# Feature-map attention and a feed-forward block on one core: hand-set slots against a list scheduler that orders all work

## The chip, the cores and the metric

The kernel runs on one core of one Trainium2 chip. Its engines run side by side: PE (TensorE, matrix multiplications), DVE (VectorE), ACT (ScalarE), POOL (GpSimd), and SP, which here only issues DMAs. Each executes its own list of instructions strictly in the order of the program and waits on semaphores for the others. The metric is the device time of one execution in microseconds (us), the median of several runs.

## The reference

Inputs are q, k, v of 8 batches, 8 heads, 576 positions, 64 elements, a matrix omega of 128 features, and weights `w_in` (512 x 2048) and `w_out` (2048 x 512), which arrive as float64.

```
phi(x) = exp(h - max(h)) / sqrt(128),  h = x @ omega.T - |x|^2/2      (x: q or k, scaled by 64**-0.25)
kv = phi(k).T @ v        z = sum over positions of phi(k)             (per batch and head)
attn = (phi(q) @ kv) / (phi(q) @ z + 1e-6)
x = attn as (4608 tokens, 512);   out = gelu(x @ w_in) @ w_out
```

A batch is 576 tokens, and its 8 heads fill the 512 columns of x. So no token of a batch can enter the feed-forward part before all heads of that batch are done.

## The kernel before, in words

**Attention** is cut into 32 units: unit k is batch k // 4 and a pair of heads, j = k % 4. Each unit loads q, k and v, projects k and q with omega on PE, subtracts the row maxima and takes exp (DVE, ACT, POOL), forms kv and z (PE), and divides numerator by denominator on DVE (`div`), which writes columns j of x. Units of batches 0 and 1 are *plain*: float32 matmuls. Those of batches 2 to 7 are *split*: each operand is divided into a high and a low part, which gives cheaper matmuls and more work for the other engines. Units share their buffers (`et`, `kvz`, `qh`), mostly single ones.

**Weights** come in 16 pieces of 1 MB through two buffers `raw`. Each is turned from float64 into float32 (ACT L199 and L203, DVE L209 and L210, POOL L215, result `w32`) and its maximum is taken (L226). When all pieces of a matrix are in, its scale follows, and each of its 16 chunks is split into two float16 halves (`wih`, `wil`; `woh`, `wol`; ACT L235, DVE L250).

**Feed-forward** goes by blocks of tokens, `TBS = (384,) * 10 + (128, 384, 256)`, and in each block by 16 chunks c of 128 hidden features. Block 0 needs no split weights: it multiplies float32 x by float32 `w32` (L937, L989). From block 1 on x is split into `xh` and `xl` (ACT L920, DVE L925, scaled by an exponent that needs the whole batch), the first product takes 12 float16 matmuls a chunk (`mm1`, L953), ACT computes gelu and its high half (L966, L967), DVE its low half `gl` (L976), and the second product takes three matmuls for every 128 tokens of a chunk (`mm2`, L995 to L997). Two PSUM buffers `h` hold first products and are free again after `gl`.

**What sets the order.** Every step is entered as an event with a time: `at(t, fn, ...)`. The times are slots of the feed-forward part (`slot`: 6 per chunk of 384 tokens) plus hand-set offsets from the table `X` (an attention unit's steps lie at fixed distances from a *burst*, one for each unit), and 37 single events are moved by `ADJ`. The events are sorted by time, and in that order the instructions are written out; each engine's list follows from it.

Of the kernel before, what the change touches and what calls it, by code (L numbers as in the profile page):

```python
# [21 lines left out]
SUB = 6  # L22
# [19 lines left out]


TBS = (384,) * 10 + (128, 384, 256)


ADJ = {6: 1.3, 24: -0.12, 25: 0.23, 27: -0.86, 44: -1.17, 46: -0.95, 64: 3.26, 65: -0.06, 67: -0.35,
# [7 lines left out]
def favor_attention_ffn(ctx: ExitStack, tc: tile.TileContext, qT, kT, v, omT, w_in, w_out, out):  # L55

# [26 lines left out]
    MID = S // P  # L83

# [16 lines left out]
    wmax = cp.tile([P, 2, NF // 2], F32, name="wmax")  # L101
    vmax = cp.tile([P, B * NJ], F32, name="vmax")
# [19 lines left out]
    def ps_at():  # L122
        return pp.tile([P, 512], F32, tag="at", name="at", bufs=3)

    def ps_h():
        return pp.tile([P, 512], F32, tag="h", name="h", bufs=2)

    def ps_acc():
        return pp.tile([P, 512], F32, tag="acc", name="acc", bufs=3)

    rot = [0]

    def ps_any():
        rot[0] += 1
        return (ps_at, ps_h, ps_acc, ps_at, ps_acc, ps_h, ps_at, ps_acc)[rot[0] % 8]()

    events = []

    def at(t, fn, *a):
        events.append((t + ADJ.get(len(events), 0), len(events), fn, a))  # L140

    class Obj:
        pass

    own = {}

    def has(u, *ks):
        assert all(own[k] is u for k in ks), (u.b, u.j, ks)

    done, steps = set(), {}  # L150

    def step(o, k):

        assert steps.get(o, 0) == k, (o, k)
        steps[o] = k + 1

    def need(*ks):
        assert all(k in done for k in ks), ks


    wi_raw = w_in.bitcast(I32).rearrange("(j p) w -> p j w", p=P)
    wo_raw = w_out.bitcast(I32).rearrange("(c p) w -> p c w", p=P)
    ep, mp, dp, late = [], [], [], []
    lent = set()

    def p2():

        if not late:
            dp.pop()
            stage.close()  # L170
            pool = ctx.enter_context(tc.tile_pool(name="p2", bufs=1, side="right", reuse_waits="tile"))
            vb = pool.tile([P, NV, VW + 1], F16, name="vb")
            nc.vector.memset(vb[:, :, D:D + 1], 1.0)
            nc.vector.memset(vb[D:P, MID, D:D + 1], 0.0)
            nc.vector.memset(vb[0:D, MID + 1, D:D + 1], 0.0)
            late.extend((pool, vb))
        return late[0]

    def w_load(pc):
        pc.raw = dp[0].tile([P, 2 * pc.n], I32, tag="raw", name="raw", bufs=2)  # L180
        for h, src in enumerate(pc.src):
            dst = pc.raw[:, h * pc.n:(h + 1) * pc.n]
            nc.sync.dma_start(dst.rearrange("p (j w) -> p j w", j=NJ) if pc.win else dst, src)
        pr = pc.raw.rearrange("p (n t) -> p n t", t=2)
        pc.lo, pc.hi = pr[:, :, 0], pr[:, :, 1]

    def w_scale(pc):
        step(pc, 0)


        if X['lsp'] >> (pc.win * 8 + pc.i) & 1 and not (pc.i > 3 and not pc.win):
            k = (pc.win, pc.i + 4) if pc.i < 4 else (False, pc.i)
            assert steps.get(('b',) + k) is None
            pc.l, pc.at = w32[:, k[0], 2 * k[1]:2 * k[1] + 2].rearrange("p c w -> p (c w)"), k
            lent.add(k)
        else:
            pc.l, pc.at = pc.lo, None
        hf = pc.hi.bitcast(F32)
        nc.scalar.activation(hf, hf, AF.Copy, scale=2.0 ** -112)  # L199
        if X['wls'] >> pc.i & 1:  # L200
            nc.gpsimd.tensor_scalar(pc.l, pc.lo.bitcast(U32), 2.0 ** -29, 1.0, op0=ALU.mult, op1=ALU.mult)
        else:
            nc.scalar.activation(pc.l, pc.lo.bitcast(U32), AF.Copy, scale=2.0 ** -29)  # L203

    def w_bits(pc):
        step(pc, 1)
        assert (pc.win, pc.i) not in lent
        step(('b', pc.win, pc.i), 0)
        nc.vector.tensor_scalar(pc.b, pc.hi, 3, None, op0=ALU.logical_shift_left)  # L209
        nc.vector.scalar_tensor_tensor(pc.b, pc.hi, -2 ** 31, pc.b, op0=ALU.bitwise_and, op1=ALU.bitwise_or)  # L210

    def w_round(pc):
        step(pc, 2)

        nc.gpsimd.tensor_tensor(pc.b, pc.b, pc.l, op=ALU.add)  # L215
        lent.discard(pc.at)
        done.update(('w32', pc.win, c) for c in pc.c)

    def w_max(pc):
        step(pc, 3)  # L220
        need(*[('w32', pc.win, c) for c in pc.c])
        if X['wmx'] >> pc.i & 1 and not pc.win:

            nc.scalar.activation(wol[:, 2 * pc.i:2 * pc.i + 2].rearrange("p c w -> p (c w)"), pc.w, AF.Abs, accum_out=wmax[:, pc.win, pc.i:pc.i + 1])
        else:
            nc.vector.tensor_reduce(wmax[:, pc.win, pc.i:pc.i + 1], pc.w, axis=AX.X, op=ALU.max, apply_absolute_value=True)  # L226
        done.add(('wmax', pc.win, pc.i))

    def w_high(pc):
        step(pc, 4)  # L230
        need(('wsc', pc.win))
        s = wsc[:, pc.win, 1:2]
        for x, (w, wh, _) in enumerate(pc.parts):
            if (pc.c[x] % 2, True, False, pc.c[x] % 4 > 0)[X['whp']]:
                nc.scalar.activation(wh, w, AF.Copy, scale=s)  # L235
            else:
                nc.gpsimd.tensor_scalar(wh, w, s, 1.0, op0=ALU.mult, op1=ALU.mult)

    def w_low(pc):
        step(pc, 5)  # L240
        s = wsc[:, pc.win, 1:2]
        for x, (w, wh, wl) in enumerate(pc.parts):
            if pc.c[x] % 4 >= 4 - X['wlp' if pc.win else 'wlq']:
                for h in range(4):
                    t = sp.tile([P, P], F32, tag="wt", name="wt", bufs=1)
                    a, d, e = (y[:, h] if pc.win else y[:, h * P:(h + 1) * P] for y in (w, wh, wl))
                    nc.gpsimd.tensor_scalar(t, a, s, 1.0, op0=ALU.mult, op1=ALU.mult)
                    nc.gpsimd.tensor_tensor(e, t, d, op=ALU.subtract)
# [123 lines left out]
    def xs_pieces(b, half):  # L372
        t0 = b * S + half * HS
        t1 = t0 + HS
        for n in range(NBLK):
            a, e = max(t0, T0[n]), min(t1, T0[n + 1])
            if a < e:
                yield n, a - T0[n], e - T0[n], a - t0
# [859 lines left out]
```

## Time and profile before

| | us |
|---|---|
| time, median of 3 runs (1007.23 to 1007.65) | 1007.6 |
| span of the profiled execution, first to last instruction | 1003.8 |
| outside the span | 3.8 |
| PE busy | 977.9 |
| DVE busy | 727.7 |
| ACT busy | 720.9 |
| POOL busy | 331.3 |

The time of the profiled execution is its span and what lies around it; the page gives the span. A matmul's recorded duration overlaps the next one's, because PE works on several at once, so busy PE is not PE at its peak. What a stream of matmuls costs is read from the distance between the starts of two records; a row of the timeline that ends in "x8" merges eight records. A float32 matmul is two records.

### The profile page before, as it was taken

The page shows a single profiled execution, that of the slowest core. Times are in us where ns is not written, and L with a number is a line of the kernel's source. Part 1 is how long each engine was busy: PE and PEld are TensorE (multiplying, and loading weights), DVE is VectorE, ACT ScalarE, POOL GpSimd, SP SyncE. Part 2 cuts the span into 40 slices and gives each one's busy share as a digit, 9 for nine tenths or more (in the row PEclk, how much of TensorE's full clock was granted, in tenths as well). Part 3 has the DMA queues.
Part 4 walks back from the last instruction along what each step waited for, and adds up shares of the span by engine and source line. Part 5 has one row for each costly group of instructions (what it writes and reads, how often), then busy time and mean ns, then how long its engine had stood idle before and what let it go on. Part 6 is the DMA issues. An engine that isn't in the chain of part 4 may idle for free.

```text
span 1003.8 us, 17322 instructions
## 1 busy us (share of the span) xinstructions
PE 977.9 (97%) x5980; PEld 597.4 (60%) x5980; DVE 727.7 (72%) x1800; ACT 720.9 (72%) x1542; POOL 331.3 (33%) x528
## 2 busy tenths in 40 slices
PE   9999999999999999899999999899999999999998
PEld 6655555566656666466566666456655656565576
DVE  5898777977778888887888779777878877431111
ACT  6876668877777877977787877877788886552333
POOL 1334314323353444343444443443454332100000
PEclk9999999999999999999999999999999999999999
DMA  8766312611211231111421222021121010000000
GB/s 245 211 211 195 120 47 61 186 43 30 79 48 48 80 100 48 43 38 48 121 58 48 69 67 72 24 77 48 49 79 43 26 59 2 22 23 1 1 32 22
DMA packets 50647, 70.91 MB, mean 71 GB/s; under 512 B 18560, under 2 KB 27136, under 8 KB 50560
## 3 DMA queue, kind: packets, MB, share of 16 engines
q1 hardware_dynamic: 50560, 69.81, 24.1%
q8 instruction: 47, 0.77, 0.3%
q14 instruction: 40, 0.33, 0.1%
HBM read 60.36 MB, written 9.44 MB: 70 GB/s over the span
## 4 chain that ended last, share of the span: by engine, by line
PE 75%; ACT 11%; DVE 8%; POOL 3%; issue 2%; DMA 1%; SPq 0%; ACTq 0%; POOLq 0%; DVEq 0%
PE h L953 29%; PE acc L995 10%; PE acc L996 10%; PE acc L997 10%; PE at L712 3%; PE at L445 2%; PE at L479 2%; PE at L632 2%; ACT xh L920 1%; POOL w L215 1%; PE h L937 1%; PE at L816 1%; PE acc L989 1%; ACT gh L967 1%; PE at L777 1%
## 5 line engine op out<-in xcount | busy, mean ns | idle before, releaser
L953 PE MATMUL h<-xh,wih 128*128 128x384 f16 (+2 forms) x768 | 238.3, 314 | 4.9 <-DVE gl L976 4.9
L953 PE MATMUL h<-xl,wih 128*128 128x384 f16 (+2 forms) x768 | 238.2, 313 | 0.0
L953 PE MATMUL h<-xh,wil 128*128 128x384 f16 (+2 forms) x768 | 237.9, 313 | 0.0
L438 POOL TENSOR_TENSOR r<-xt,r 64x256 fp32r<-64x256 f32 (+2 forms) x216 | 164.8, 770 | 216.0 <-ACT r L432 209.4
L995 PE MATMUL acc<-woh,gh 128*128 128x512 f16 (+1 forms) x528 | 198.7, 377 | 0.4 <-ACT o L1006 0.4
L996 PE MATMUL acc<-woh,gl 128*128 128x512 f16 (+1 forms) x528 | 198.4, 376 | 0.1
L997 PE MATMUL acc<-wol,gh 128*128 128x512 f16 (+1 forms) x528 | 198.4, 376 | 0.0
L953 PEld LDWEIGHTS <-wih 128*128 128x128 f16 x1536 | 142.9, 98 | 85.6 <-DVE gl L976 3.3
L976 DVE SCALAR_TENSOR_TENSOR gl<-h,bs,gh 128x384 f16<-128x384 f32 (+2 forms) x192 | 110.7, 578 | 112.2 <-ACT gh L967 109.3
L966 ACT ACTIVATE h<-h,bs 128x384 f32<-128x384 f32 (+2 forms) x192 | 100.9, 527 | 95.6 <-PE h L953 94.4
L432 ACT CAST r<-xt 128x256 fp32r<-128x256 f32 (+2 forms) x216 | 84.6, 404 | 43.1 <-PE at L479 23.3
L967 ACT ACTIVATE gh<-h,bs 128x384 f16<-128x384 f32 (+2 forms) x192 | 105.8, 553 | 3.4
L953 PEld LDWEIGHTS <-wil 128*128 128x128 f16 x768 | 75.2, 98 | 47.4 <-issue 4.6
L997 PEld LDWEIGHTS <-gh 128*128 128x128 f16 x544 | 53.2, 98 | 60.3
L995 PEld LDWEIGHTS <-gh 128*128 128x128 f16 x544 | 52.9, 97 | 43.8 <-ACT gh L967 0.2
L996 PEld LDWEIGHTS <-gl 128*128 128x128 f16 x544 | 53.3, 98 | 41.3 <-issue 0.7
L445 PE MATMUL at<-om,r 128*128 128x256 f32 x216 | 60.5, 352 | 1.5 <-DVE et L464 0.8
L479 PE MATMUL at<-r,om 128*128 128x288 f32 x192 | 56.1, 374 | 1.3 <-DVE et L464 0.8
L725 ACT ACTIVATE dt<-at,vsc 64x288 f32<-64x288 f32 x80 | 39.6, 495 | 21.5 <-PE at L712 20.2
L732 DVE STREAM_TRANSPOSE rt<-dt 128x288 f32<-128x288 f32 x64 | 30.4, 475 | 29.0 <-ACT dt L725 25.7
L550 ACT CAST qh<-qt 128x288 fp32r<-128x288 f32 x96 | 40.5, 433 | 13.5 <-DVE qt L543 13.3
L937 PE MATMUL h<-xs,w 128*128 128x384 f32 x128 | 47.7, 499 | 0.8 <-ACT g L960 0.6
(196 smaller groups left out, 1810.4 us busy)
## 6 DMA issues: line engine op xcount, KB each, us to landing
xt<-in_kT SPq DMA_DIRECT2D x56, 288.0 KB, 4.0
xt<-in_qT SPq DMA_DIRECT2D x56, 288.0 KB, 3.9
out_x<-o SPq DMA_DIRECT2D x35, 256.0 KB, 2.0
raw<-in_w_in SPq DMA_DIRECT2D x16, 512.0 KB, 5.0
raw<-in_w_out SPq DMA_DIRECT2D x16, 512.0 KB, 4.5
w<-in_v SPq DMA_DIRECT2D x5, 1280.0 KB, 7.2
vt<-in_v SPq DMA_DIRECT2D x12, 320.0 KB, 4.1
out_x<-o SPq DMA_DIRECT2D x2, 128.0 KB, 1.7
```

The lines of the kernel that those rows point to most:

```text
L432: nc.scalar.copy(u.r[i][:, 0:b - a], xf[:, a:b])
L438: nc.gpsimd.tensor_tensor(r, xf[D:, a:b], r, op=ALU.subtract)
L445: nc.tensor.matmul(u.pp[i][:, t], r[:, t * P:(t + 1) * P], om, start=True, stop=True)
L479: nc.tensor.matmul(ps[:, 0:HS], om[:, i], r, start=(i == 0), stop=(i == 1))
L937: nc.tensor.matmul(hs[0, c][:, 0:TB[0]], wi32[:, c, j], xs[0, j][:, 0:TB[0]], start=(j == 0), stop=(j == NJ - 1))
L953: nc.tensor.matmul(h[:, 0:TB[n]], w, (xh, xh, xl)[k], start=(i == 0), stop=(i == 3 * NJ - 1))
L966: nc.scalar.activation(g, h, AF.Gelu, scale=bsc[n][:, 2:3])
L967: nc.scalar.activation(gh, g, AF.Copy, scale=bsc[n][:, 3:4])
L976: nc.vector.scalar_tensor_tensor(gl, g, bsc[n][:, 3:4], gh, op0=ALU.mult, op1=ALU.subtract)
L995: nc.tensor.matmul(acc, gh[:, s], woh[:, c, c0:c1], start=(c == 0), stop=False)
L996: nc.tensor.matmul(acc, gl[:, s], woh[:, c, c0:c1], start=False, stop=False)
L997: nc.tensor.matmul(acc, gh[:, s], wol[:, c, c0:c1], start=False, stop=(c == NF - 1))
```

## The change

The table of offsets, the moved events and the sorting are gone. Every step is now an operation `op(engine, cost, function, ..., r=, w=, new=)`: it names what it reads and writes and which new buffers it takes. From that the class `Planner` derives dependencies. Each operation gets a due time, going backwards from its successors, from tables `STARTS` (a time for each block) and `UDUE` (one for each half of each unit), and an offset by kind of step (`OFF`). `Planner.run` then keeps a clock for each engine: whenever an engine is free, it takes, of all operations that are ready and whose buffers are free, the one with the earliest due time. The instructions are written out in that order, before the kernel runs, and pinned on each engine with order-only dependencies (`add_manual_dep`).

The blocks are now `(256, 256) + (384,) * 10 + (256,)`: 13 as before, the float32 block 0 with 256 tokens, and blocks 0 and 1 (512 tokens) lie inside batch 0. The x of both is one tile `xa`. Units 1 and 3 of the first batch use second copies of `et`, `kvz` and `qh` (laid over the place where `w_out` will stand, `flat0`), the first four units may take any of the eight PSUM buffers as they are free, and plain units load q and k into alternating halves of `xt`. The weights' pieces are all of `w_in` first, then all of `w_out`; before, they alternated. What is computed stays the same, step by step.

```
-TBS = (384,) * 10 + (128, 384, 256)
+TBS = (256, 256) + (384,) * 10 + (256,)
...
-    def at(t, fn, *a):
-        events.append((t + ADJ.get(len(events), 0), len(events), fn, a))
...
-    for t, _, fn, a in sorted(events, key=lambda e: e[:2]):
...
-        fn(*a)
+        for o in reversed(self.ops):
+            k, n, x, add = o.own or (0, 0, 0.0, 0.0)
+            o.due = 1e9 if k == 0 else UDUE[n] if k == 2 else add if k == 3 else add + STARTS[n] + ...
+            for s in o.succ:
+                o.due = min(o.due, s.due - o.c - (lat.get(o.e, 0) + hop.get(s.e, 0) if s.e != o.e else 0))
...
+                for o in cand[e]:
+                    t = room(o)
+                    if t is None:
+                        continue
+                    if t > now + 1e-9:
+                        later.append(t)
+                        continue
+                    p = (o.due - bonus.get(o.kind, 0.0), o.id)
+                    if best is None or p < best[0]:
+                        best = (p, o)
...
+            u.eb = j % 2 if b == 0 else int(u.mode == 2 and j % 2 == 0 and u.k > X['eb0'])
...
+    xa = cp.tile([P, NJ, TB[0] + TB[1]], F32, name="xa")
+    qh2 = flat0[:, 2 * NT * M:2 * NT * M + R2]
...
+    def put(o):
+        n = len(nc.cur_bb.bb.instructions)
+        o.fn(*o.a)
+        for i in nc.cur_bb.bb.instructions[n:]:
+            if i.engine in last:
+                tc.add_manual_dep(i, last[i.engine], ...)
```

Three places show how the order moves. The first is PE's list at the end of the float32 block, where the first split block begins. Before (`xs` is x, `acc` a second product, `w` the float32 weights, `et` and `r` parts of an attention unit):

```order
L989 MATMUL acc<-w_71,g 128x512
L479 MATMUL at<-r,om 128x288 x2
L937 MATMUL h<-xs_0_272,w_71 128x384
L937 MATMUL h<-xs_1_418,w_71 128x384
L445 MATMUL at<-om,r 128x256
L937 MATMUL h<-xs_2_516,w_71 128x384
L703 MATMUL at<-qh,kvz 64x288 x4
L937 MATMUL h<-xs_3_624,w_71 128x384
L479 MATMUL at<-r,om 128x288 x2
L989 MATMUL acc<-w_71,g 128x512 x3
L479 MATMUL at<-r,om 128x288 x2
L953 LDWEIGHTS wih
L953 MATMUL h<-xh,wih 128x384
```

and now:

```order
L1035 MATMUL acc<-w_71,g 128x512 x5
L554 MATMUL at<-vt_73,et 128x65 x8
L554 MATMUL at<-vt_73,et 128x130
L1009 MATMUL h<-xa,w_71 128x256 x4
L592 MATMUL at<-ident,et 128x128 x4
L523 MATMUL at<-om_66,xt 128x128 x8
L592 MATMUL at<-ident,et 128x128 x4
L1014 LDWEIGHTS wih
L1014 MATMUL h<-xh,wih 128x256
L1014 LDWEIGHTS wil
L1014 MATMUL h<-xh,wil 128x256
```

The float32 matmuls have 256 columns instead of 384, and the first split block, also of 256 columns, starts while plain units of batch 1 (`om,xt`, `ident,et`) are still in work; before, the last plain unit was just ending (`qh,kvz`) and split units had begun (`r,om`).

The second is DVE's list at the last `xl` of the first block that needs batch 1: block 1 before, block 2 now. Before:

```order
L733 RECIPROCAL rc<-rt 128x9
L490 TENSOR_REDUCE mx<-et 128x9
L734 STREAM_TRANSPOSE rt<-rc 128x288
L250 SCALAR_TENSOR_TENSOR wol<-w_71,wsc,woh 128x512
L740 TENSOR_TENSOR xs_3_642<-at,rt 128x192
L740 TENSOR_TENSOR xs_3_1481<-at,rt 128x96
L488 STREAM_TRANSPOSE et<-at 128x288
L250 SCALAR_TENSOR_TENSOR wol<-w_71,wsc,woh 128x512
L925 SCALAR_TENSOR_TENSOR xl<-xs_3_642,bs,xh 128x384
```

and now:

```order
L761 TENSOR_TENSOR et<-at,lo 128x256
L762 TENSOR_REDUCE nm<-et 128x2
L805 TENSOR_TENSOR ql<-qt,qh 128x288
L1030 SCALAR_TENSOR_TENSOR gl<-h,bs,gh 128x256
L799 STREAM_TRANSPOSE qt<-et 128x288
L805 TENSOR_TENSOR ql<-qt,qh 128x288
L579 RECIPROCAL zr<-zr 128x2
L580 TENSOR_REDUCE km<-at 128x2
L1003 SCALAR_TENSOR_TENSOR xl<-xs,bs,xh 128x384
```

Before, 283 DVE instructions stand up to that `xl`, seven splits of `w_out` (`wol`) are still to come after it, and no `gl` has been computed. Now 347 stand there, among them all sixteen `wol`, fifteen `gl` of block 1, eight maxima of v, and the end of a first split unit (`qt`, `ql`).

The third is DVE's list at a later block's start. Before, at block 4:

```order
L976 SCALAR_TENSOR_TENSOR gl<-h,bs,gh 128x384
L925 SCALAR_TENSOR_TENSOR xl<-w_71,bs,xh 128x384
L732 STREAM_TRANSPOSE rt<-dt 128x288
L488 STREAM_TRANSPOSE w_71<-at 128x288
L733 RECIPROCAL rc<-rt 128x9
L490 TENSOR_REDUCE mx<-w_71 128x9
L734 STREAM_TRANSPOSE rt<-rc 128x288
L925 SCALAR_TENSOR_TENSOR xl<-w_71,bs,xh 128x384
L743 TENSOR_TENSOR w_71<-at,rt 64x288 x2
L502 TENSOR_TENSOR mx<-mx,mc 64x36
L976 SCALAR_TENSOR_TENSOR gl<-h,bs,gh 128x384
```

and now, at block 5, the one that needs batch 3 as block 4 did:

```order
L1003 SCALAR_TENSOR_TENSOR xl<-w_71,bs,xh 128x384 x2
L773 STREAM_TRANSPOSE w_71<-at 128x288
L775 TENSOR_REDUCE mx<-w_71 128x9
L761 TENSOR_TENSOR w_71<-at,lo 128x256
L762 TENSOR_REDUCE nm<-w_71 128x2
L834 SCALAR_TENSOR_TENSOR w_71<-et,w_71 128x256 x2
L761 TENSOR_TENSOR w_71<-at,lo 128x128
L762 TENSOR_REDUCE nm<-w_71 128x1
L834 SCALAR_TENSOR_TENSOR w_71<-et,w_71 128x256
L1030 SCALAR_TENSOR_TENSOR gl<-h,bs,gh 128x384
L773 STREAM_TRANSPOSE w_71<-at 128x288
L1030 SCALAR_TENSOR_TENSOR gl<-h,bs,gh 128x384
```

Before, block 4's `xl` stand one by one between the last `gl` of block 3, with division and maxima of attention units between them. Now they come at up to two in a row and are spread over a longer stretch of attention work, with the `gl` in pairs.

More of the change, by code (lines that the diff above doesn't have):

```diff
@@ L157, in need @@
[L157 to L177, printed above, removed]
@@ L219, in w_max @@
[L219 to L237, printed above, removed]
@@ L239, in w_low @@
[L239 to L248, printed above, removed]
-            else:
-                nc.vector.scalar_tensor_tensor(wl, w, s, wh, op0=ALU.mult, op1=ALU.subtract)
-        done.update(('w', pc.win, c) for c in pc.c)
@@ new lines, in favor_attention_ffn @@
+    ANY = ('at', 'acc', 'h')
+    op('SP', 0, load_om, w=['om32'], size=65e3)
+    op('DVE', 0.6, zeros, w=['z', 'ones', 'vt1s', ('w32', 0, NF - 1)])
+    op('PE', 4.8, warm, r=['z', ('w32', 0, NF - 1)], new=[('h', 'warm')], due=(3, 0, 0.0, -50.0))
+    op('POOL', 0.5, identity, w=['ident'])
+    op('DVE', 0.23, scale_om, w=['om32'])
+    op('DVE', 0.5, split_om, r=['om32'], w=['om'])
+    wi_raw = w_in.bitcast(I32).rearrange("(j p) w -> p j w", p=P)
+    wo_raw = w_out.bitcast(I32).rearrange("(c p) w -> p c w", p=P)
@@ new lines, in v_scales, with v_spread, batch_v @@
+    def v_scales(b):
+        t = G['vsc', b]
+        fields(vexp[:, 0, b:b + 1], t[0:32])
+        mul(nc.gpsimd, t[0:32, 1:2], t[0:32, 0:1], EPS * KSC)
+    def v_spread(b):
+        spread(G['vsc', b])
+    def batch_v(b):
+        us = units[b * NJ:(b + 1) * NJ]
+        op('SP', 0, load_vst, b, w=[u.vk for u in us], size=1311e3)
+        for u in us:
+            op('DVE', 0.8, v_max, u, r=[u.vk], w=[('vm', b)])
+        chain(b, 0)
+        op('POOL', 0.8, v_scales, b, r=[('exp', b, 0)], new=[('vsc', ('vsc', b))])
+        op('ACT', 0.3, v_spread, b, w=[('vsc', b)])
@@ L1202, in favor_attention_ffn, with block @@
[L1202 to L1206 removed]
+    mp.append(ctx.enter_context(tc.tile_pool(name="mp", bufs=1, reuse_waits="tile")))
+    def block(n):
+        block_prep(n)
+        for c in range(NF + LAG):
+            if c < NF:
+                ffn_first(n, c)
+            if c >= LAG:
+                ffn_second(n, c - LAG)
@@ new lines, in favor_attention_ffn @@
+    for u in units[:NJ]:
+        unit_plain(u)
+    chain(0, 1)
+    op(None, 0, nothing, deps=[o for u in units[1:NJ:2] for k in (('kvz', u), ('qh', u)) for o in PL.users[k]],
+       w=[('w32', 0, c) for c in range(8)] + [(x, 1, t) for x, n in (('et', NT), ('eq', 4)) for t in range(n)])
+    for i in range(NF // 2):
+        weights_in(1, i)
+    for i in range(NF // 2):
+        weights_in(0, i)
+    op('DVE', 0.2, p2, w=['p2', 'vb'], deps=[o for w in range(2) for i in range(NF // 2) for o in PL.users['raw', w, i]])
@@ new lines, in favor_attention_ffn @@
+    for c in range(NKK, NF):
+        op(None, 0, nothing, w=[('w32', 1, c), ('xw', c)])
+    done_u = NJ
+    for n in range(1, NBLK):
+        b1 = (T0[n + 1] - 1) // S
+        while done_u < (b1 + 1) * NJ:
+            u = units[done_u]
+            if u.j == 0 and not u.kp:
+                batch_v(u.b)
+            (unit_split if u.split else unit_plain)(u)
+            done_u += 1
+            if u.j == NJ - 1:
+                chain(u.b, 1)
+        block(n)
+    lat = dict(PE=0.18, ACT=0.107, DVE=0.07, POOL=0.046)
```

1549 lines of the change are left out of this document (756 added, 793 removed), and 8 rows, old and new, of tables (ADJ, UDUE).

## The prediction

> **What bounds the kernel now.** I read the page first, then the table by stretches of time, the groups of matmuls, the timeline and the waits.
>
> ```profile
> span 1003.8 us, 17322 instructions
> PE 977.9 (97%) x5980; PEld 597.4 (60%) x5980; DVE 727.7 (72%) x1800; ACT 720.9 (72%) x1542; POOL 331.3 (33%) x528
> PE 75%; ACT 11%; DVE 8%; POOL 3%; issue 2%; DMA 1%; SPq 0%; ACTq 0%; POOLq 0%; DVEq 0%
> ```
>
> PE looks full, but the chain that ended last spends a quarter of the span on other things. So PE's queue and PE's waits both count. What a full stream costs is read from starts in the timeline of PE (start, duration, line, out<-in, shape, count), first in the float32 block, then in a 384-token and in a 256-token block:
>
> ```profile
> 141.06 2.74 PE L937 MATMUL h<-xs,w 128*128 128x384 f32 x8
> 143.73 1.19 PE L703 MATMUL at<-qh,kvz 128*64 128x288 f32 x8
> 144.85 2.84 PE L989 MATMUL acc<-w,g 128*128 128x512 f32 x6
> 147.53 1.45 PE L937 MATMUL h<-xs,w 128*128 128x384 f32 x4
> ...
> 900.07 0.33 PE L953 MATMUL h<-xh,wih 128*128 128x384 f16 x1
> 902.02 0.38 PE L995 MATMUL acc<-woh,gh 128*128 128x512 f16 x1
> ...
> 957.81 0.27 PE L953 MATMUL h<-xh,wih 128*128 128x256 f16 x1
> 959.12 0.38 PE L995 MATMUL acc<-woh,gh 128*128 128x512 f16 x1
> 961.07 0.27 PE L953 MATMUL h<-xh,wih 128*128 128x256 f16 x1
> ...
> 1000.37 0.27 PE L997 MATMUL at<-wol,gh 128*128 128x256 f16 x1
> ```
>
> Twelve float16 matmuls of 384 columns take 902.02 - 900.07 = 1.95 us, 0.163 each; twelve of 256 columns 1.31, 0.109 each; nine of 512 columns 1.95, 0.217 each. Float32 records take 2.67 / 8 = 0.334 (384 columns) and 2.68 / 6 = 0.447 (512 columns), changes of kind included. The counts stand in the groups of PE by shape:
>
> ```profile
> L953 PE MATMUL h<-xh,wih 128*128 128x384 f16 x640 | 209.3, 327 | 4.9 <-DVE gl L976 4.9
> L995 PE MATMUL acc<-woh,gh 128*128 128x512 f16 x512 | 194.3, 380 | 0.4 <-ACT o L1006 0.4
> L445 PE MATMUL at<-om,r 128*128 128x256 f32 x216 | 60.5, 352 | 1.5 <-DVE et L464 0.8 <-POOL r L438 0.7
> L479 PE MATMUL at<-r,om 128*128 128x288 f32 x192 | 56.1, 374 | 1.3 <-DVE et L464 0.8 <-POOL r L438 0.5
> L937 PE MATMUL h<-xs,w 128*128 128x384 f32 x128 | 47.7, 499 | 0.8 <-ACT g L960 0.6 <-DVE xs L740 0.2
> L989 PE MATMUL acc<-w,g 128*128 128x512 f32 x96 | 45.7, 598 | 0.0
> ```
>
> Three groups of 640 and three of 512 like the first two rows are 1920 x 0.1625 + 1536 x 0.217 = 645 us; charging every other group in the same way by its closest spacing (the smaller blocks 42, the float32 block 82, attention 171, the warm-up 5) brings the 5980 records to 945. Of the span, 59 us are no stream of matmuls, more than the 26 of visible idle. Charged by stretches, some 31 of the 59 lie before 190 us, 24 between there and 1000, and 3.4 behind the last matmul.
>
> The table by stretches (start:end, length, then busy time and count of PE, PEld, DVE, ACT, POOL, the granted clock, DMA) shows who is short where:
>
> ```profile
> 0.00:25.00 25.00, 22.62 (x186) 17.12 (x187) 13.72 (x38) 16.83 (x47) 4.15 (x8) 1.00 0.85 245
> 25.00:175.00 150.00, 144.41 (x750) 83.97 (x749) 123.99 (x247) 109.48 (x198) 52.08 (x52) 1.00 0.47 142
> 250.00:400.00 150.00, 148.08 (x901) 91.48 (x899) 123.56 (x325) 115.86 (x260) 64.13 (x108) 1.00 0.25 68
> 400.00:550.00 150.00, 145.05 (x882) 87.21 (x880) 124.17 (x321) 121.45 (x267) 62.79 (x106) 1.00 0.22 60
> ```
>
> The granted clock is 1.00. In 25:175 PE executes 750 records, in 250:400 901; DVE is 83% busy in both. At the start no engine is full: the work waits for weights and for one unit at a time. Later it is the blocks' starts:
>
> ```profile
> PE h L953 <- DVE gl L976: 4.9, 6, 1.4
> PE at L632 <- POOL w L609: 3.7, 4, 1.1
> ...
> 406.82 0.92 DVE L743 TENSOR_TENSOR w<-at,rt 64x288 f32<-64x288 f32 x2
> 407.77 0.19 DVE L502 TENSOR_TENSOR mx<-mx,mc 64x36 f32<-64x36 f32 x1
> 407.99 0.62 DVE L976 SCALAR_TENSOR_TENSOR gl<-h,bs,gh 128x384 f16<-128x384 f32 x1
> 408.53 0.61 DVE L925 SCALAR_TENSOR_TENSOR xl<-w,bs,xh 128x384 f16<-128x384 f32 x1
> ...
> 408.67 0.34 PE L953 MATMUL h<-xh,wih 128*128 128x384 f16 x1 [1.15 <-DVE gl L976]
> ```
>
> Block 4's first matmul at 408.67 waits 1.15 us for a `gl` that stands on DVE behind two divisions; the last attention steps of a batch, the new block's `xh` and `xl` and the old one's `gl` all want the same moment.
>
> **The change part by part.** *Fewer float32 tokens.* For 128 tokens the float32 block spends (128 x 0.334 + 96 x 0.447) / 3 = 28.6 us, or 27.5 by the closest spacing. These tokens move into float16: the block of 128 becomes one of 256. That adds half of 192 x 0.109 + 96 x 0.217, 20.9 us. PE gains 6.6 to 7.7; I take **7**. Other matmuls are the same in number, as are table loads of ACT up to two, so nothing else is removed; DVE has 24 small divisions more (more blocks cut through a unit's tokens), with 24 x about 0.2 = 5 us, beside PE.
>
> The Trainium skill ("TensorE: Matmul & The Clock Gate", back-to-back issue gap) gives two figures for 512 columns, 216 ns by a formula and about 131 ns as the sustained spacing of real streams. By 131 the 48 second products of the added tokens would cost 6.3 instead of 10.4, and the gain would be about 11. This trace has 217, so the sum stays with it.
>
> *The start.* Before, the first split block reaches into batch 1 and needs eight units. Now block 1 ends at token 512 and needs batch 0 alone; block 2 is the first that needs eight units. The comparable points are PE's first matmul of block 1 before and of block 2 now:
>
> ```profile
> 171.16 0.34 PE L953 MATMUL h<-xh,wih 128*128 128x384 f16 x1
> ...
> 173.59 0.61 DVE L925 SCALAR_TENSOR_TENSOR xl<-xs,bs,xh 128x384 f16<-128x384 f32 x1
> ```
>
> Up to there PE's list before amounts to 140 us of stream, reached at 171, so 31 short. Now it holds 77 - 55 = 22 less of the float32 block and 41 more of block 1 and further units: 159. On DVE 283 instructions stand up to that last `xl`, with 137 us busy (the two stretches' 13.72 + 123.99) and 37 idle. Now it is 347 instructions; the 64 more are priced by DVE's groups:
>
> ```profile
> L976 DVE SCALAR_TENSOR_TENSOR gl<-h,bs,gh 128x256 f16<-128x256 f32 x16 | 7.8, 484 | 35.6 <-ACT gh L967 35.6
> L250 DVE SCALAR_TENSOR_TENSOR wol<-w,wsc,woh 128x512 f16<-128x512 f32 x16 | 12.2, 781 | 0.4 <-ACT woh L235 0.4
> L851 DVE TENSOR_REDUCE vmax<-w 128x1 f32<-128x640 f32 x20 | 15.5, 798 | 0.0
> ```
>
> Fifteen `gl` 7.3, seven `wol` 5.5, eight maxima 6.4, and about 10 for parts of split units: 29, of which consecutive instructions overlap a tenth: 27. So DVE must be busy for 164 us before that `xl`, against 159 of PE's stream. **DVE now sets the time of block 2's start**, and its idle time decides: at least the 11 us of the first 25, in which data arrive, at most the 37 it has now. PE is then 164 + 11 - 159 = 16 to 42 short there. A second copy of the first units' tiles and free choice of ready work should remove waits behind a blocked instruction. That eight maxima of v, needed only by batches 3 and 4, stand so early shows that the planner found room on DVE there. But dependencies stay, so I keep 12 of the 26 idle us after the first 25 (DVE 92% busy): 164 + 11 + 12 = 187, 28 short, where PE before is 31 short at the same amount of stream. Gain **3** (bounds -11 and +15).
>
> `w_in` now comes wholly ahead of `w_out` in SP's queue. Up to the last piece of `w_out` there are 16.8 MB of weights and about 7 of q, k, v; at the 245 GB/s of the first stretch that is 97 us, at a fifth less 121, and block 1's second products begin after 118 us of stream and 16 or more of shortfall. The order is covered by that; without the cover it would cost some 10 us for a splitting that can't begin before the last piece is in.
>
> *Later blocks.* Of the 24 us I count some 18 at block starts and 6 as the spread loss of changing between float16 and attention matmuls, which stays. Before, new batches are needed at blocks 1, 3, 4, 6, 7, 9, 11; now at 2, 3, 5, 6, 8, 9, 11, so the starts of 4 and 7, where it waits longest, get free, and 5 and 8 take over their need. A due time for each `gl` and `xl` should shorten waits like the one at 408.67; a planner's clock that is off by a few tenths of a us makes new ones. Bounds: all 18 gone, or 10 more (half again as many). I take **10** gained. The tail (last store) is the same.
>
> Sum: 1003.8 - 7 - 3 - 10 = 983.8, and with the 3.8 by which the median stands above the span, **987.6**.
>
> **The rivals.** *(a) DVE becomes the bound.* Before, DVE reaches its place in the list at a steady rate: 83% busy in each stretch up to 550. If that is set by dependencies which a scheduler can't remove, the early 37 idle us remain, block 2 starts 42 short, 11 more than now, and since block 3 needs 12 units at token 896 (before at 1152) DVE stays behind until block 3's `xl`, for some 8 us more; the later starts gain nothing. 1007.6 - 7 + 11 + 8 = 1020 at most, and about 1014 if a third of the 19 is made up. With the 8 it decides from the point at which DVE is idle for over 27 us ahead of block 2's `xl`. For it: DVE's list is front-loaded now. Against it: a ready list leaves an engine idle only if nothing is ready.
>
> *(b) Only the matmuls count*: the new order waits as often as the old one. 1007.6 - 7 = 1001.
>
> *(c) The scheduler works nearly perfectly*: 16 short at block 2 instead of 31 and 18 gone later, 1007.6 - 7 - 15 - 18 = 968.
>
> *(d) The order isn't executed as planned* (the pinned lists wait at places where the planner's clock is wrong by much): no change within 2 us, with losses that eat the 7.
>
> **How the numbers follow.** Forecast 0.55, its own range 976 to 998; (a) 0.14, (b) 0.15, (c) 0.13, (d) 0.03. The range of 8 in 10 leaves out the slower half of (a) and the faster half of (c): 968 to 1010. A measurement of this kernel tells about 0.2% (2 us) from no change: faster 0.83 (forecast, b, c), the same 0.04, slower 0.13.
>
> **What would show it.** The PE groups should have 64 float32 matmuls (128 records) of 256 columns at about 0.22 between starts, and 64 records fewer of 512 (right for the 7). The first 384-column float16 matmul should start near 187; near 175 speaks for (c), near 200 for (a), with DVE about 92% busy between 25 and 175 in the forecast and 83% in (a). Later, the waits of L953's successor on `gl` should fall from 4.9 to under 3, and a stretch such as 400:550 should hold fewer than 3 us of PE idle instead of 5. The forecast is wrong if PE's idle in the middle rises, or if PE's stream up to block 2 isn't behind DVE but behind ACT or the DMAs of `w_out`.

## The result

The change takes 1009.6 us (median of 20 runs, 1007.7 to 1013.2) against 1007.1 for the kernel before (20 runs, 1004.9 to 1011.2): a ratio of 1.0033, 95% interval 1.0020 to 1.0046. It is 0.3% slower, where 987.6 us and a gain of 2% were forecast. The profiled execution spans 1006.9 us, before 1003.8.

The page of the change, the lines that answer to those of before (span, busy time by engine, the granted clock, which is the share of its full speed that PE's clock was allowed, in tenths for 40 slices, and the chain of waits by engine):

```profile
span 1006.9 us, 17394 instructions
PE 973.8 (97%) x5996; PEld 606.1 (60%) x5996; DVE 777.6 (77%) x1824; ACT 724.7 (72%) x1538; POOL 341.6 (34%) x528
PEclk7999999999999999999999999999999999999999
PE 77%; DVE 13%; ACT 3%; POOL 2%; DMA 2%; issue 2%; SPq 1%; ACTq 0%; POOLq 0%; DVEq 0%
```

PE is busy for 4 us less. DVE has 24 instructions more and is busy 50 us longer (727.7 before), and its share of the chain that ended last goes from 8% to 13%. So DVE's groups come next, by shape. First the kernel before, then the change (count, busy us, mean ns of one):

```profile
L925 DVE SCALAR_TENSOR_TENSOR xl<-w,bs,xh 128x384 f16<-128x384 f32 x28 | 17.4, 640 | 8.3 <-ACT xh L920 5.8 <-POOL bs L908 2.0 <-PE h L953 0.5
L250 DVE SCALAR_TENSOR_TENSOR wil<-w,wsc,wih 128x512 f16<-128x512 f32 x16 | 11.9, 776 | 2.0 <-ACT wih L235 2.0
L510 DVE TENSOR_TENSOR nq<-mx,mc 32x36 f32<-32x36 f32 x24 | 4.1, 170 | 0.1
```

```profile
L1003 DVE SCALAR_TENSOR_TENSOR xl<-w,bs,xh 128x384 f16<-128x384 f32 x36 | 29.3, 840 | 3.2 <-ACT xh L999 3.2
L403 DVE SCALAR_TENSOR_TENSOR wil<-w,wsc,wih 128x512 f16<-128x512 f32 x16 | 16.8, 1083 | 0.0
L787 DVE TENSOR_TENSOR nq<-mx,mc 32x36 f32<-32x36 f32 x24 | 8.1, 336 | 0.5 <-ACT mc L784 0.5
```

The same instructions, of the same shapes, take 31%, 40% and 98% longer on average. A mean hides that most of them are as before and a few are several times as long. The timeline shows three of these with what POOL does at the time (start, duration, engine, line, out<-in):

```profile
106.74 3.54 DVE L403 SCALAR_TENSOR_TENSOR wil<-w,wsc,wih 128x512 f16<-128x512 f32 x2
106.95 2.79 POOL L381 TENSOR_TENSOR w<-w,raw 128x1024 int32<-128x1024 int32 x1 [3.74 <-DVE w L378]
...
119.95 2.40 POOL L381 TENSOR_TENSOR w<-w,raw 128x1024 int32<-128x1024 int32 x1 [10.22 <-DVE w L378]
120.07 2.84 DVE L375 TENSOR_SCALAR w<-raw 128x1024 int32<-128x1024 int32 x1
...
744.33 2.62 POOL L766 TENSOR_TENSOR w<-w,nm 128x1152 f32<-128x1152 f32 x1 [0.18 <-PE h L1014]
744.90 2.47 DVE L1003 SCALAR_TENSOR_TENSOR xl<-w,bs,xh 128x384 f16<-128x384 f32 x1
```

Each long DVE instruction begins while a POOL instruction runs and ends 0.42 to 0.55 us after that one's end, which is less than its own usual 0.61 to 0.74. The first of the two `wil` in the first row is a normal one; the second starts at 107.40 and takes 2.88. DVE is **held** until POOL is done. I add up, for each kind of DVE instruction, what single ones take over the usual (the 20th percentile of the kind), counting those with 250 ns or more (below, "holds" are these): 8 instructions with 5.7 us before, **40 with 31.3 us in the change**.

Which pairs do this can be read from one profile, by taking every DVE instruction that begins while POOL is in one (change; mean us that POOL's instruction still had to run, and mean us that DVE's took over its usual):

```
DVE instruction (tensors it reads)         while POOL runs   cases   left   over
block_low, L1003 (two in SBUF)             k_shift  L766        5    1.64   1.46
w_low, L403 (two in SBUF)                  w_round  L381        3    2.03   1.84
q_low, L805 (two in SBUF)                  x_low    L740       10    0.41   0.30
w_shift, L375 (one in SBUF, 1024 columns)  w_round  L381        3    0.95   0.82
proj_add, L761, L762 (at most one in SBUF) x_low    L740      156    0.40   0.00
q_blocks, L773, L775 (at most one)         k_shift  L766       54    1.08   0.00
```

Instructions with two inputs in SBUF are held for nearly all that is left; those with one from PSUM (L761, L773), and reductions (L762, L775), not at all. It goes the other way too: 12 `x_low` of POOL that began during a `q_shift` of DVE took 0.68 us more, of 0.79 left.

**The plan and the chip.** The planner computes a start for each operation. Set beside the trace, these show where the plan is lost. Its end is 978.0 us, so the chip is 28.9 behind. By the starts of mm1, PE is about 1 us late up to 100 us of the plan, 7 late at 110, 9 at 200, 17 near 490, 22 near 605, 28 at 727. The first step lies at the two `wil` of 2.85 and 2.88 us; the later ones at the `xl` (`block_low`) of 496.6, 512.6, 631.3 and 744.9 us, each held by a `k_shift`. The planner's clock knows prices, latencies between engines and buffers. It has no wait between DVE and POOL.

### The profile page after: what moved, and what is told of

Same layout as the page of the kernel before. It is cut to its first block, busy times and chain, and to the rows that moved or that the text cites. A ratio compares the mean times of both kernels' runs of the same rounds, so it can differ in the third digit from the quotient of the medians.

```text
span 1006.9 us, 17394 instructions
## 1 busy us (share of the span) xinstructions
PE 973.8 (97%) x5996; PEld 606.1 (60%) x5996; DVE 777.6 (77%) x1824; ACT 724.7 (72%) x1538; POOL 341.6 (34%) x528
## 4 chain that ended last, share of the span: by engine, by line
PE 77%; DVE 13%; ACT 3%; POOL 2%; DMA 2%; issue 2%; SPq 1%; ACTq 0%; POOLq 0%; DVEq 0%
PE h L1014 31%; PE acc L1038 9%; PE acc L1040 9%; PE acc L1039 9%; PE at L611 3%; PE at L770 2%; PE at L748 2%; PE at L554 2%; DVE xl L1003 1%; PE acc L1035 1%; PE at L845 1%; PE h L1009 1%; DVE gl L1030 1%; DMA vt<-in_v 1%; DVE wil L403 1%
## 5 line engine op out<-in xcount | busy, mean ns | idle before, releaser
L1014 PE MATMUL h<-xh,wih 128*128 128x384 f16 (+1 forms) x768 | 244.9, 319 | 5.9 <-DVE gl L1030 5.5
L740 POOL TENSOR_TENSOR r<-xt,r 64x288 fp32r<-64x288 f32 (+2 forms) x216 | 168.0, 795 | 228.1 <-ACT r L735 161.1
L1014 PE MATMUL h<-xh,wil 128*128 128x384 f16 (+1 forms) x768 | 245.0, 319 | 0.0
L1014 PE MATMUL h<-xl,wih 128*128 128x384 f16 (+1 forms) x768 | 244.8, 319 | 0.0
L1030 DVE SCALAR_TENSOR_TENSOR gl<-h,bs,gh 128x384 f16<-128x384 f32 (+1 forms) x192 | 112.7, 588 | 125.5 <-ACT gh L1026 123.2
L1022 ACT ACTIVATE h<-h,bs 128x384 f32<-128x384 f32 (+1 forms) x192 | 102.6, 535 | 75.8 <-PE h L1014 72.4
L1026 ACT ACTIVATE gh<-h,bs 128x384 f16<-128x384 f32 (+1 forms) x192 | 107.6, 561 | 67.8 <-PE acc L1040 54.9
L1014 PEld LDWEIGHTS <-wil 128*128 128x128 f16 x768 | 75.3, 98 | 52.8 <-issue 11.2
L662 DVE TENSOR_TENSOR w<-at,rt 64x128 f32<-64x128 f32 (+6 forms) x168 | 54.3, 323 | 3.2
L802 ACT CAST qh<-qt 128x288 fp32r<-128x288 f32 x96 | 40.2, 428 | 11.4 <-DVE qt L799 9.5
L381 POOL TENSOR_TENSOR w<-w 128x1024 int32<-128x1024 int32 x12 | 28.7, 2391 | 53.1 <-DVE w L378 29.1
L805 DVE TENSOR_TENSOR ql<-qt,qh 128x288 fp32r<-128x288 f32 x96 | 44.9, 482 | 1.8 <-ACT qh L802 1.6
```

The lines of the kernel that those rows point to most:

```text
L662: nc.vector.tensor_tensor(x[r, c0:c1], ps[r, r0:r1], rt[r, r0:r1], op=ALU.mult)
L740: nc.gpsimd.tensor_tensor(r, xf[D:, a:b], r, op=ALU.subtract)
L1014: nc.tensor.matmul(h[:, 0:t], w, (G['xh', n, j], G['xh', n, j], G['xl', n, j])[k][:, 0:t], start=(i == 0), stop=(i == 3 * NJ - 1))
L1022: nc.scalar.activation(h, h, AF.Gelu, scale=G['bs', n][:, 2:3])
L1026: nc.scalar.activation(G['gh', n, c][:, 0:t], G['h', n, c][:, 0:t], AF.Copy, scale=G['bs', n][:, 3:4])
L1030: nc.vector.scalar_tensor_tensor(G['gl', n, c][:, 0:t], G['h', n, c][:, 0:t], G['bs', n][:, 3:4], G['gh', n, c][:, 0:t], op0=ALU.mult, op1 ...
```

## The experiments

Three theories. **H** (held): these waits, which the planner's clock lacks, took the gain. **S** (start): the loads and the 4.05 us in which PE waits at 14.9 us, with the lower clock behind it, set the start, and the rest follows. **C** (prices): the plan is missed because its prices are too low here and there. All kernels compute what the change computes unless the expectation says what is left out.

**1 to 3. POOL writes in place of its largest reads.** The order of every engine is kept; three operations of POOL are replaced by writes of about their length (the edits, shortened). Its smaller ones still read SBUF.

```
 def w_round(pc):
-    nc.gpsimd.tensor_tensor(pc.b, pc.b, pc.l or raw(pc)[1], op=ALU.add)
+    tensor_tensor(pc.b[:, 0:8], pc.b[:, 0:8], lo[:, 0:8], add)
+    memset(lo, 0); memset(lo, 0)
+    tensor_tensor(pc.b[:, 0:8], pc.b[:, 0:8], lo[:, 0:8], add)
 # second and third kernel also:
 def x_low(u, i):
-    nc.gpsimd.tensor_tensor(r, xf[D:, a:b], r, op=ALU.subtract)
+    three memsets of r, together as long
 def k_shift(u):
-    nc.gpsimd.tensor_tensor(es, es, nm..., op=ALU.add)
+    nc.gpsimd.memset(es, 0.0); nc.gpsimd.memset(es, 0.0)
```

`w_round` alone:

> The change with its order kept, but POOL's w_round (16 of 2.4 us) only writes: two memsets of the low half's buffer between two additions of 8 columns, so that it takes about as long as before (left out: the rounding's low bits in 1016 of 1024 columns; the data is otherwise the same). Theory H (held): DVE instructions with two SBUF inputs are held while a POOL instruction that reads SBUF runs; the planner's clock has no such wait. Then the two w_low of 2.85 and 2.88 us and the w_shift of 2.84 us become 0.72 to 0.85 us, block 2's first mm1 comes at 192 us in place of 200.8 (9 us earlier, an estimate from the planner's clock played over this order with the wait added), and the span falls by 7 to 10 us, to 997 to 1000. Theory S (the start's loads and the 4.05 us that PE waits at 14.9 us set the start): block 2 stays at 199 to 201 us and the span within 2 us of 1006.9. Theory C (the plan is missed because its prices are too low here and there): the same as S.

Measured: 1002.1 us, ratio to before 0.9949 (0.9922 to 0.9976), span 1001.7. The two `w_low` of 2.85 and 2.88 us take 0.75 and 0.74, the `w_shift` of 2.84 takes 0.68, and the holds fall from 31.3 to 25.3 us. The time is 7.5 us under the change by the medians; the profiled span is 5.2 us under it, where H named 7 to 10. S and C are out by more than they allow. Block 2's first mm1 stands at 196.5 us and gained 4.3 us, not 9: in this execution PE is already 2.3 us behind the plan at 72 us (1.1 in the change), and between there and block 2 it loses another 2.6 us (8.1 in the change), whose cause I can't name.

All three:

> The change with its order kept, but POOL's three largest reads of SBUF only write: w_round as in the other run, x_low as three memsets (left out: the low half of each projection input is zero), k_shift as two memsets (left out: the K features' exponents are all 0), each of about its former length. H: nearly all of the 31 us that 40 DVE instructions take over their usual time goes, block 2's first mm1 comes at 192 us, the PE gaps near 503, 625, 751 and 766 us close, and the span falls to 980 to 986 (the planner's clock played over this order: 984 with these three reads gone, 978 without any hold). S: the span stays over 1000. C: it falls by less than 5 us, since prices that are too low stay too low.

Measured: 991.3 us, ratio 0.9843 (0.9817 to 0.9868), span 989.2, **18.4 us under the change with the same order on every engine**. One held instruction is left, with 0.7 us. With the wait and the low clock of the start still there this is far beyond what S and C allow. The groups that were long are back (the lines are shifted by 5 to 7):

```profile
L1010 DVE SCALAR_TENSOR_TENSOR xl<-w,bs,xh 128x384 f16<-128x384 f32 x36 | 21.0, 610 | 3.3 <-ACT xh L1006 3.2
L408 DVE SCALAR_TENSOR_TENSOR wil<-w,wsc,wih 128x512 f16<-128x512 f32 x16 | 11.3, 738 | 0.0
L794 DVE TENSOR_TENSOR nq<-mx,mc 32x36 f32<-32x36 f32 x24 | 4.1, 170 | 0.5 <-ACT mc L791 0.5
```

PE's gaps of 1.4, 2.4 and 1.0 us at 503, 751 and 766 us are gone; behind 100 us two of 0.4 us or more are left, the longer 0.65. Some 3 to 9 us are missing from what H expected; 11.2 us behind the plan remain without holds, taken up below. Most of that is at the start: **block 2's first mm1 stands at 198.5 us, not 192**, only 2.3 us earlier than in the change. PE was 4.3 us behind the plan at 72 us already, and the granted clock was 0.50 from 55 to 65 us (0.80 and 0.86 in the change); from 72 us to block 2 it loses 2.6 us, like the run before.

The control:

> The same three edits in the kernel before, its order kept: a control. H: there only 8 DVE instructions were held, for 5.7 us together, so the time falls by 1 to 6 us, to about 1002 to 1006. If the memsets made either kernel faster in a way of their own (shorter POOL work, fewer waits for its results), this one would gain 15 us or more, like the change.

Measured: 1000.2 us, ratio 0.9938 (0.9918 to 0.9958): 6.7 us gained, somewhat more than the 1 to 6 that H named, and far from the change's 18.4. The holds fell by 3.6 us, to 3 with 2.1 us, so some 3 us of the gain are not holds of this size; the 18 us are not what the memsets give by themselves. The hand-set order had few holds to lose. (POOL's reads are still needed, so neither kernel is a version to use.)

These two runs also compare the two orders with nearly all holds gone: 991.3 against 1000.2 us. There the change's order is **8.9 us faster**; with POOL's reads it is 2.5 us slower. So the reads cost the new order 11.4 us more than the old one, and of the forecast gain of 20 us some 11 are missing even without them.

**4. The wait in the planner's clock.**

```
+    lock = dict(DVE=0.0, POOL=0.0)                 # in Planner.run
     ... emit:
+    if o.e in lock and o.fn.__name__ in SHARED:
+        lock[o.e] = t + c - (0.12 if o.e == 'DVE' else 0.18)
     ... room:
+    if o.e in lock and o.fn.__name__ in SHARED:
+        t = max(t, lock[OTHER[o.e]])
```

> The change with the wait in the planner's clock: an instruction of DVE or POOL on a list of those that use two SBUF inputs (DVE) or read SBUF (POOL) can't be taken while the other engine has one in work, so the planner takes another one or waits; its constants are those of the change, which were set without the wait, and its clock ends at 1004.8 us (978.0 in the change). H: the sum of what DVE's instructions take over their usual time falls from 31 us to under 8 us; the chip now ends within 5 us of the plan, at a span of 1000 to 1009 (28.9 us behind the plan in the change). C: the chip ends 20 to 30 us behind the plan again, at 1025 to 1035. S: no statement on the plan; the start is as late as in the change.

Measured: 1016.2 us, ratio 1.0089 (1.0061 to 1.0116), span 1014.5: 9.7 us behind the plan, not 28.9. H named 5 at most and C at least 20, so H is nearer, but out too. From 75 to 275 us PE stays within about 0.7 us of the plan; from there to 965 us it falls 12 us behind. Holds: 26 with 16.1 us, not under 8; with the wait in the clock, some are planned (nothing else is ready). But it is a worse plan: its constants were found for another clock. Knowing the wait isn't the same as having an order that avoids it.

**5. The start kept busy.**

```
 def q_trans(u, g):
+    for i in range(18 * (u.k == 0 and g == 0)):
+        nc.tensor.matmul(G['pt', u, g][:, 0:256], z16[:, 0:P], z16, start=True, stop=True)
```

> The change with 18 more matmuls of zeros (128x256 bf16, into the tile that unit 0's first q_trans fills next) ahead of that q_trans, where PE otherwise waits 4.05 us from 10.8 to 14.9 us; all else as in the change. In the profile of the change the granted clock is 0.50 and 0.61 in the two stretches of 5 us after that wait. Theory S (the wait and the clock behind it set the start): the clock stays at 1.00, block 2's first mm1 comes 3 to 5 us before 200.8, and the time falls by 3 to 5 us. Theory H (held DVE): the clock stays at 1.00, but DVE, not PE, sets the pace there (9.3 to 9.6 of 10 us busy from 30 to 50 us), and against the plan the change's PE is only 0.5 us late at 90 us; so block 2 comes at most 1.5 us earlier, and the time changes by less than 2 us. The sum of DVE's holds stays near 31 us.

Measured: 1009.7 us, ratio 1.0025 (1.0010 to 1.0039), the same as the change; block 2 at 202.5, holds 31.3 us. So filling this wait gains nothing. It is no clean test of S, though: both theories were wrong on the clock (table by stretches; the figure behind POOL's is the granted clock), which stayed higher here and fell later instead:

```profile
15.00:20.00 5.00, 3.84 (x27) 3.36 (x26) 2.81 (x6) 5.00 (x14) 2.61 (x2) 0.89 1.04 266
20.00:25.00 5.00, 5.00 (x40) 3.89 (x39) 4.12 (x8) 4.17 (x17) 2.26 (x2) 0.77 1.10 306
60.00:65.00 5.00, 5.00 (x25) 4.43 (x26) 3.19 (x11) 1.88 (x5) 0.86 (x1) 0.50 0.17 40
```

At 30 us of the plan DVE is 1.7 us earlier against it than in the change, at 70 us 1.6 us later. What speaks against S is the run with all three edits: there block 2 comes only 2.3 us earlier, and the time falls by 18.4.

**6. One part undone: single tiles.**

```
-u.eb = j % 2 if b == 0 else int(...)        # and kvz2, qh2 for units 1 and 3
+u.eb = 0 if b == 0 else int(...)
```

> The change with one part undone: the first batch's units have one set of et, kvz and qh tiles (eb = 0 for b = 0, no kvz2 and qh2) and the planner orders anew with its constants as they are. By the planner's clock, which has no holds, block 2's first mm1 is planned at 195.5 us (191.6 in the change) and the end at 987.8 (978.0). H: the chip ends 20 to 40 us behind this plan again, at a span of 1008 to 1028, with 25 us or more of DVE instructions held. S (the start decides and the rest follows the plan): 10 us over the change, a span of 1015 to 1018, all of it there before block 2. If the double tiles did nothing: a span within 3 us of 1006.9.

Measured: 1026.4 us, ratio 1.0198 (1.0183 to 1.0213), span 1025.3, 37.5 behind its plan, 58 held with 43.1 us. Block 2 comes at 204.8, 4.0 later than in the change (plan: 3.9). So with this scheduler and these constants the double tiles are worth 17 us, 4 of them at the start; 12 of the rest is the difference in holds, since any new order meets POOL at other places. S named a span of 1015 to 1018. It is no measure of the tiles alone.

**7 and 8. The deciding pair.** Both have new prices, both had their constants searched for the same time from the same start, and both plans end at the same time. Only one clock knows the wait.

```
-num 0.8, proj_q 0.27, rcp 0.92, proj_add 0.17 + ..., q_blocks 0.78, ...
+num 0.85, proj_q 0.30, rcp 1.12, proj_add 0.23 + ..., q_blocks 0.86, ...   # both
+lock as in experiment 4                                                    # one
+STARTS, UDUE, OFF and bonuses searched anew with each clock                # both
```

> The change with the wait between DVE and POOL in the planner's clock, prices of 17 kinds of operation set to what the change's trace shows (PE num 0.85 in place of 0.80, proj_q 0.30 for 0.27, DVE rcp 1.12 for 0.92, proj_add +0.06, q_blocks 0.86 for 0.78; w_shift, q_low, exps, g_high and others lower), and the constants STARTS, UDUE, OFF and the five bonuses searched anew with that clock. The plan ends at 983.4 us, block 2's first mm1 stands at 192.0. H: the chip ends within 8 us of the plan, at a span of 984 to 991, DVE's holds of 250 ns or more sum to under 10 us (some are planned), and the kernel beats both the kernel before and the change. If holds were not what the plan lacked: a span of 1000 or more.

> The control to that run: the same prices, the same search for as long from the same constants, but the planner's clock has no wait between DVE and POOL. The plan ends at 983.3 us, 0.1 from the other; block 2's first mm1 stands at 196.1. H: the chip ends 25 to 45 us behind this plan, at a span of 1008 to 1028 (the plan's order played with the waits ends at 1029; for the change such a replay came out some 7 us over the chip), with 25 us or more of DVE's holds. If the prices were what the plan lacked (theory C): within 8 us of the plan, like the other run.

Measured: **994.5 us with the wait, ratio 0.9882 (0.9853 to 0.9912); 1023.8 us without, ratio 1.0162 (1.0147 to 1.0177).** The spans are 990.6 and 1022.8, for plans that end at 983.4 and 983.3. Prices alone don't make the plan come true, so C isn't the main cause; the wait does most of it. The kernel with the wait beats both kernels, by 13.5 us the one before (1007.9 in the same runs). Its holds are 26 with 17.3 us, where H named under 10; for 5.8 us of them the plan itself lets DVE wait at that place. Its four runs span 990.5 to 996.2 us, so they end 7 to 13 us behind the plan; those without the wait 38 to 39.5. Each plan comes from a single search, and how much two searches with the same clock differ wasn't tested. The pages of both (with the wait, then without):

```profile
PE 966.4 (98%) x5996; PEld 603.7 (61%) x5996; DVE 762.1 (77%) x1824; ACT 720.7 (73%) x1538; POOL 336.3 (34%) x528
PE 79%; ACT 8%; DVE 8%; issue 2%; POOL 2%; DMA 1%; SPq 1%; ACTq 0%; POOLq 0%; DVEq 0%
```

```profile
PE 977.1 (96%) x5996; PEld 605.8 (59%) x5996; DVE 786.9 (77%) x1824; ACT 723.5 (71%) x1538; POOL 340.0 (33%) x528
```

All runs together (us; holds of 250 ns or more: count, sum):

| kernel | plan's end | span | behind | holds |
|---|---|---|---|---|
| before | – | 1003.8 | – | 8, 5.7 |
| before_pool_writes | – | 998.1 | – | 3, 2.1 |
| change | 978.0 | 1006.9 | 28.9 | 40, 31.3 |
| start_kept_busy | 978.0 | 1007.9 | 29.9 | 40, 31.3 |
| wround_writes | 978.0 | 1001.7 | 23.7 | 38, 25.3 |
| pool_writes | 978.0 | 989.2 | 11.2 | 1, 0.7 |
| single_tiles | 987.8 | 1025.3 | 37.5 | 58, 43.1 |
| prices_no_wait | 983.3 | 1022.8 | 39.5 | 53, 44.6 |
| planner_knows | 1004.8 | 1014.5 | 9.7 | 26, 16.1 |
| prices_and_wait | 983.4 | 990.6 | 7.2 | 26, 17.3 |

In the orders planned without the wait, the lag follows the holds, with 11.2 us left where there are almost none: 4.3 of these are there at 72 us, 6.9 at block 2, 12 near 605. What they are isn't settled: by the change's trace a `num` takes 0.14 and a `proj_q` 0.13 us more of PE than planned (48 and 96 of them), of which the new prices of the pair take up 0.05 and 0.03, and the low clock near 60 us goes with the first 4; neither was tested by itself.

The clock is also a rival for a part of the result. The mean granted clock of the change's 20 runs is 0.983 to 0.992, and those at 0.983 span 1010.8 and 1011.2 us, those at 0.990 to 0.992 span 1006.5 to 1007.8. The kernel before was at 0.990 to 1.000 in 12 runs, and spans 1011.1 at 0.990, 1003.1 to 1004.7 at 1.000. So some us of the change may be its lower clock. It doesn't explain the experiments' differences: the run with the three edits had 0.987 to 0.990, and the pair 0.982 to 0.992 and 0.990 to 0.992.

## Why the prediction was wrong, by its own steps

*What bounds the kernel*: right as far as it went. PE's stream plus PE's waits stayed the account: charged as in the prediction, the stream fell from 945 to 938, the span rose by 3, so 69 us are no stream instead of 59.

*Fewer float32 tokens*: 7 forecast, 6.9 found. The groups have the counts that were expected, but for one: the float32 records of 512 columns fell from 96 to 64, by 32 and not by 64.

```profile
L1014 PE MATMUL h<-xh,wih 128*128 128x384 f16 x640 | 210.0, 328 | 5.2 <-DVE gl L1030 4.8
L1038 PE MATMUL acc<-woh,gh 128*128 128x512 f16 x528 | 200.9, 380 | 0.5 <-ACT o L1047 0.5
L1014 PE MATMUL h<-xh,wih 128*128 128x256 f16 x128 | 34.9, 272 | 0.7 <-DVE gl L1030 0.6
```

*The start*, **the first step that failed**: block 2's first mm1 was forecast at 187, and stands at 200.8 with 158.7 us of stream ahead: 42 short instead of 28, a loss of 11 where 3 were to be gained. Up to block 2's last `xl`, after the 347 instructions that were counted, the change, `w_round` only writing, and all three edits show (busy PE, PEld, DVE):

```profile
0.00:202.10 202.10, 183.21 (x1199) 127.95 (x1199) 172.68 (x347) 146.31 (x297) 60.91 (x67) 0.96 0.51 155
```

```profile
0.00:197.80 197.80, 180.97 (x1199) 126.63 (x1199) 166.18 (x347) 146.38 (x297) 61.70 (x115) 0.97 0.53 159
```

```profile
0.00:199.70 199.70, 185.70 (x1199) 130.15 (x1199) 165.54 (x347) 146.50 (x297) 61.50 (x144) 0.94 0.52 157
```

DVE's busy time was priced well without holds (164 against 166.2 and 165.5) and is 172.7 with them. Its idle time was the guess that failed: 29.4, 31.6 and 34.2, not 11 + 12 = 23. And "DVE now sets the time of block 2's start" isn't borne out: with the three edits DVE is busy 7.1 us less up to that `xl`, which comes only 2.4 us earlier. In the change PE never waits for 0.4 us or more between 112.1 us and block 2's first mm1. Its waits lie before, and of the four longest, three are on ACT, which is in part the sign that the prediction named for being wrong (PE's stream not behind DVE but behind ACT):

```profile
PE at L592 <- ACT et L539: 4.0, 1, 4.0
PE at L523 <- DVE kvz L563: 3.9, 1, 3.9
PE at L523 <- ACT dt L616: 2.7, 1, 2.7
PE h L602 <- ACT w L596: 2.6, 1, 2.6
```

Of the 13.8 us between 187 and 200.8, the plan itself has 4.6 (block 2 at 191.6), and the chip adds 9.2: 1.1 up to 72 us and 8.1 from there, of which 5.5 are absent when `w_round` only writes. So the holds are some 5.5 us of it, the second wait above included; the cause of the rest stays open. "A ready list leaves an engine idle only if nothing is ready" holds in the plan, not on the chip.

*`w_in` ahead of `w_out`, hidden*: right. PE's longest wait ahead of a second product is the 0.5 for ACT's store above, none for `woh` or `wol`.

*Later blocks*, **the second step that failed**: 10 forecast, 0 found. Between 200 and 800 us, 21.4 were no stream before, 21.8 in the change, and **7.3 with the three edits**. So the scheduler did remove these waits, 14 us of them, even more than forecast, and the holds put as much back: what was late next is `xl`, then the first mm1 of a block (`gl` at 751 us, 2.4 of the 5.5 us below), or POOL's `bs` (PE waits 1.4 us on it at 503 us). The step failed at "a planner's clock that is off by a few tenths of a us makes new ones": it is off by up to 2.2 us at single places.

*The rivals.* (a) gave block 2's 42 exactly, which is in part luck: it is made of DVE's holds and of 29.4 us of idle time, where (a) had 37 of idle time, and DVE's busy share isn't 83% but 89% (133.98 of 150 below). With the three edits (a) is nearer at the start than the forecast is: 34.2 us idle, block 2 40 short. Its other half, that later starts gain nothing, fits the change's number but not its cause: without the holds they gain 14. (b) and (c) are out. (d), no change within 2 us because the planner's clock is wrong by much, with a chance of 0.03, is nearest: 2.5 us. Its chance was set without asking what kind of wait the clock can't contain.

*What would show it*:

```profile
25.00:175.00 150.00, 137.09 (x876) 94.37 (x875) 133.98 (x255) 110.52 (x210) 45.23 (x40) 0.98 0.47 147
400.00:550.00 150.00, 148.10 (x898) 89.09 (x897) 135.68 (x331) 121.81 (x266) 60.25 (x107) 0.99 0.20 56
PE h L1014 <- DVE gl L1030: 5.5, 8, 2.4
```

The time near 200 spoke for (a) as written. The stretch 400:550 has 1.9 us of PE idle, under the 3 named, and still no gain came of it as a whole: one stretch was too small a sign. The waits on `gl` rose from 4.9 to 5.5 instead of falling below 3.

The sum: 7 gained as forecast; 11 lost at the start for a gain of 3; 0 for 10 later, and 1 gained outside these stretches. Of the 23 us between forecast and result (span: 983.8 against 1006.9), 17.7 go when POOL's largest reads go; but the old order gains 5.7 in the same way (1003.8 to 998.1), so 12 of the 23 go with the reads in the new order alone. The other 11 are missing at the start.

## What to carry to other kernels

A scheduler finds the order that is best in its own clock, and does nothing to avoid a wait that the clock lacks: the three orders that were planned without it had 40, 58 and 53 holds. (That a better packed plan collides more was not tested.) Compare planned and measured starts, operation by operation; the place where the lag jumps names the missing rule, and a table of "instruction began while another engine was in X" tells which pairs are concerned. Run the same edit on both kernels before a difference is put down to it: it took the holds from both, and the two orders then still weren't 20 us apart. An order that was tuned on the chip may have that rule inside without anyone having written it down (8 holds against 40).

## What was not expected of the hardware

A DVE instruction with two inputs in SBUF (0.61 to 0.74 us) took up to 2.88 us while POOL ran an instruction that reads SBUF; `proj_add`, one input from PSUM or a reduction of one SBUF tensor, was not delayed beside `x_low` (156 cases, 0.00 us). With the three edits, 4 `w_low` that began during a memset took 0.002 us over their usual with 0.74 us of it left, and 34 memsets that began during a `q_shift` 0.000. But `w_shift`, one SBUF input of 1024 columns, is held by a write as well:

```profile
105.44 0.95 POOL L386 MEMSET w<- 128x1024 int32 x1
105.56 1.38 DVE L375 TENSOR_SCALAR w<-raw 128x1024 int32<-128x1024 int32 x1
109.32 1.41 DVE L408 SCALAR_TENSOR_TENSOR wil<-w,wsc,wih 128x512 f16<-128x512 f32 x2
109.52 1.06 POOL L386 MEMSET raw<- 128x1024 int32 x1
```

(0.68 is its usual time; the two `wil` beside the second write take the usual 0.66 from start to start.) The Trainium skill ("SBUF — State Buffer", "Who interferes with whom") says that DVE and GpSimd share a pair of ports as an exclusive lock, whoever comes first blocking the other for a whole instruction: for DVE instructions in a mode that uses both ports against any GpSimd instruction, for those with two SBUF inputs only against one that reads SBUF. These runs agree for the instructions with two inputs. That `w_shift` runs in such a mode no run shows by itself; it takes 0.68 us where a `w_sign`, with two inputs of the same 1024 columns, takes 1.21. A held instruction loses some 0.1 to 0.2 us less than what is left of the other.

The granted clock of PE was 0.50 and 0.61 in the two stretches of 5 us behind a wait of 4.05 us; with that wait filled in part it was 0.89 and 0.77 there, and 0.65 and 0.50 from 55 to 65 us, behind two waits of 2.7 us that end at 50.9 and 55.9 us (the change has two like them, and 0.80 and 0.86 there). In the profiled execution of the kernel before it stays at 1.00 up to 950 us. The time was the same with and without the filling.
